# Banded attention with a gated MLP on one core: constant products taken out and the program listed in another order

## The chip, the core and the metric

The kernel runs on one core of a Trainium2 chip. The core's engines work side by side, each through its own list of instructions in the order of the program: PE (TensorE, matrix products into the eight PSUM banks), DVE (VectorE), ACT (ScalarE), POOL (GpSimd) and SP, whose queue issues the DMAs. An instruction waits on semaphores for what it reads. The metric is the device time of one execution in microseconds; lower is better.

## The reference

Attention over 8 batches and 8 heads, 576 positions, with a band of 128 keys and a bias per head; its result, heads side by side, is the input x of a gated MLP whose gate mixes along the sequence.

```python
scores = scale * q @ k.T                       # per batch and head, 576 x 576, D = 64
scores = where((rel >= 0) & (rel < 128), scores - slope[h] * abs(rel), -1e9)
x = concat_heads(softmax(scores) @ v)          # 8 x 576 x 512
h = gelu_tanh(x @ w_in)                        # 512 -> 1024
u, v = h[..., :512], h[..., 512:]
v_n = (v - mean(v)) / sqrt(var(v) + 1e-6) * g_ln
v_s = einsum('ts,bsd->btd', w_sg, v_n) + b_sg  # along the sequence
out = x + (u * v_s) @ w_out
```

## The kernel before

**Order.** All work is cut into named steps. A string, ORDER (L861 on), lists them; `plan.run` goes through it, and `pin` chains the instructions of each engine in that order. So the string sets the order on every engine, and nothing is moved later. A set of names, ON_VECTOR (L66), says which copies and subtractions run on DVE; the others run on ACT (copies) or POOL (subtractions).

**Attention.** A "two" d (0 to 15, two for each batch) holds four heads. Its steps: q (load q and k of two heads, L250), `*a *b *c` (scores, 48 PE instructions each, L287), `A` and `B` (add the bias and take the row minima, DVE, L320), `e` and `E` (exps, ACT, L324), `R` (sum and reciprocal, DVE, L328 and L329), `s` and `z` (scale, POOL, L337, L342), `t` (transpose, DVE, L351), `Va` and `Vb` (product with v, PE, L383). `La` and `Lb` load `vt`, the values of a batch (L264, L266). The q tiles have two buffers apart from the second two, so q4 and q5 wait for the scores of the first two.

**Into the MLP.** For each pair of heads n (four a batch): x (gather from PSUM, L405, L409), h (round to the upper half, L414), l (the rest, the lower half, L417), k (copy of its tail, L420). All products of the MLP are made of three: upper by upper, upper by lower, lower by upper (L628, L629, L630).

**Weights.** `w_in` comes in eight pieces and `w_out` in four, numbered 0 to 11, as 64-bit floats that the core takes apart: i (load into one of four `wst` buffers, L184), r and d (three ACT instructions, L196, L200, L202), b (DVE, L204), + (POOL, L206; it frees the buffer), H (round, L208), - (lower half, L210). 0 to 3 belong to the v-half of `w_in`, 4 to 7 to the u-half, 8 to 11 to `w_out`. The spatial weights: wl, wH, w- for four pieces, tl, tH, t- for the tail, bl, bH, b- for the bias.

**MLP of batch b.** v-sums (`v`; in batch 0 in pieces w and v, one for each pair), vg (gelu, ACT), nv..b, p, c, h and vn (norm: DVE, POOL, DVE, ACT, DVE), tt, tj, tg, nt, tn (the tail of 64 rows), u-sums and uc (copy to SBUF), ug (one gelu over all of u, 2.1 us on ACT), y-sums (along the sequence, L628 to L630, L777, L778; the first of them needs every vn, tn and w-), gm (gate, DVE), gh and gl (halves, ACT and POOL), O (`w_out`), oa (add x, DVE), D (store). u, y and O steps are named by batch, column block and half of the sequence.

**Constant products.** Steps K0 to K23 are listed, and those in ON_VECTOR (ten) issue six products of a constant with itself into an idle PSUM bank (L574), which nothing reads.

Of the kernel before, what the change touches and what calls it, by code (L numbers as in the profile page):

```python
# [22 lines left out]
def attention_gmlp(  # L23
# [833 lines left out]
    for b in range(B):  # L857
# [8 lines left out]
        bH q6 H4 k1 w22 nv10c w01 nv10p -4 v00 b- nv10h k3 q7 k2 w21 w30 vn01 i5 v02 vg00 nv00b vg02 nv20b nv00c
        nv20c w32 La1 nv00p *c3 nv20p *b3 Rb2 Ea2 ea2 nv00h Ra2 w31 Bc3 sb2 vn00 nv20h vn02 tb2 ec2 v03 vg03 sa2
        nv30b nv30c r5 d5 b5 tl i7 Ac3 ta2 tH tt0 nv30p K15 nv30h Rc2 +5 wl1 H5 vn03 -5 tj0 tg0 Bb3 nt0b Lb1 wl0
        sc2 z2 nt0c nt0p *a3 tc2 wH0 ec3 nt0h K6 Va2 Ab3 tn0 r7 q8 Vb2 Aa3 d7 t- Ba3 x4 b7 +7 x6 eb3 H7 -7 w-0
        q9 K10 *a4 *c4 Eb3 wH1 *b4 u020 Rb3 Ba4 Bb4 sb3 w-1 Ea3 Ec3 u010 i9 ea3 u000 Ab4 u001 u021 r9 uc000 Rc3  # L870
        Ra3 q11 wl2 Aa4 Ea4 wl3 uc020 Bc4 tb3 uc001 uc010 u031 sa3 z3 d9 u030 i11 wH3 sc3 uc031 r11 Ac4 uc021
        tc3 ta3 u011 uc030 b9 Eb4 h6 w-3 wH2 d11 Ec4 Va3 Vb3 +9 x5 w-2 y011 b11 +11 y030 q10 y020 l6 h5 ec4
        uc011 H9 x7 H11 y001 l5 *a5 i10 ug0 h4 y021 y031 h7 eb4 gm030 l7 i8 gm021 ea4 gm011 -11 gm031 -9 l4 gh03
        *c5 y010 gm020 Aa5 r8 r10 d10 gh02 k6 gl02 k4 d8 *b5 k5 Ba5 y000 Ac5 gm001 v12 b8 b10 K13 k7 Ab5 +8 +10
        gl03 Ea5 gm010 tt1 ea5 u120 gm000 v10 H8 Rb4 Bb5 gh01 H10 u100 -10 gh00 q13 -8 gl01 sb4 eb5 tj1 u121 K14
        Bc5 La2 Ra5 gl00 tg1 ec5 uc100 tb4 nt1b nt1p Rc4 nt1c q12 Oa00 Ec5 nt1h u131 O000 Lb2 O020 v13 Rc5 Eb5
        tn1 vg10 uc120 oa020 nv01b vg13 z4 O021 O011 Oa01 K17 u110 oa021 sa5 sc4 nv31b nv01c nv31p nv31c nv01p
        oa011 Rb5 nv01h uc110 vn10 Ra4 u130 u111 O031 nv31h K9 vn13 O001 uc121 uc131 ta5 sa4 oa000 uc130 uc111
        vg12 v11 ta4 oa001 tc4 vg11 oa031 nv11b nv21b Va4 D00 O030 Vb4 sb5 oa030 tb5 D02 z5 nv21p nv11c x10 u101
        sc5 nv11p x8 nv11h tc5 *a6 nv21c uc101 ug1 vn11 Ba6 Aa6 *c6 h10 Va5 O010 h8 Vb5 l8 Bc6 k8 oa010 nv21h  # L880
        vn12 D01 Ac6 y100 x9 y130 Ea6 *b6 D03 q14 x11 ec6 h9 l10 y110 l9 ea6 gm100 gm110 Ab6 Ec6 y101 k9 y131
        gm130 q15 *b7 *c7 gm101 h11 l11 k11 k10 Ra6 y121 tt2 Bb6 Ac7 y111 Ab7 Rc6 tj2 gm131 tg2 nt2b y120 *a7
        nt2p gh10 Bb7 v20 Eb7 gm120 sa6 Eb6 eb6 u200 gm121 Aa7 Ba7 v23 sc6 nt2c gm111 gl10 gh11 u221 gh13 gh12
        nt2h ea7 eb7 gl12 gl11 u230 ta6 v22 gl13 Ea7 Rb6 uc200 tn2 Oa10 vg22 nv22b Oa11 O130 uc221 O100 O101
        nv22c z6 La3 O121 nv22p nv22h vg23 vn22 oa100 u201 nv32b oa101 uc230 sb6 v21 O111 Ra7 Bc7 q16 O120 vg20
# [84 lines left out]
```

## Time and profile before

| | us |
|---|---|
| median of three runs | 608.28 (604.44 to 609.07) |
| the profiled execution | 603.53 |
| its span, first to last instruction | 601.8 |
| PE busy | 571.9 (95%) |
| DVE, ACT, POOL busy | 364.9, 347.6, 219.0 |

An fp32 product of attention stands in the trace as two PE instructions' records, and the ends of matmuls are modelled. The profile gives the granted TensorE clock as a share of full speed (1.00 is 2.4 GHz, 0.50 is 1.2 GHz).

### The profile page before, as it was taken

The page shows a single profiled execution, that of the slowest core. Times are in us where ns is not written, and L with a number is a line of the kernel's source. Part 1 is how long each engine was busy: PE and PEld are TensorE (multiplying, and loading weights), DVE is VectorE, ACT ScalarE, POOL GpSimd, SP SyncE. Part 2 cuts the span into 40 slices and gives each one's busy share as a digit, 9 for nine tenths or more (in the row PEclk, how much of TensorE's full clock was granted, in tenths as well). Part 3 has the DMA queues.
Part 4 walks back from the last instruction along what each step waited for, and adds up shares of the span by engine and source line. Part 5 has one row for each costly group of instructions (what it writes and reads, how often), then busy time and mean ns, then how long its engine had stood idle before and what let it go on. Part 6 is the DMA issues. An engine that isn't in the chain of part 4 may idle for free.

```text
span 601.8 us, 20210 instructions
## 1 busy us (share of the span) xinstructions
PE 571.9 (95%) x8632; PEld 525.4 (87%) x8632; DVE 364.9 (61%) x1253; ACT 347.6 (58%) x948; POOL 219.0 (36%) x206
## 2 busy tenths in 40 slices
PE   9668789998999999999999999999999999999997
PEld 9557579888988899988989899998998899999997
...
GB/s 262 122 189 89 208 136 178 49 116 71 40 43 134 93 21 80 103 104 3 78 83 133 3 112 101 104 84 1 101 62 127 59 9 55 23 0 1 1 40 118
DMA packets 27085, 50.22 MB, mean 83 GB/s; under 512 B 2674, under 2 KB 17010, under 8 KB 26996
## 3 DMA queue, kind: packets, MB, share of 16 engines
...
## 4 chain that ended last, share of the span: by engine, by line
PE 84%; DVE 6%; ACT 4%; DMA 3%; issue 2%; SPq 1%; POOL 0%; ACTq 0%
PE bank L628 21%; PE bank L629 20%; PE bank L630 20%; PE bank L383 9%; PE bank L287 6%; PE bank L574 3%; DMA vt<-v_in 2%; PE bank L778 1%; PE bank L777 1%; DMA qk<-qkT 1%; DVE e L320 1%; PE bank L711 1%; PE bank L713 1%; DVE wo L210 1%; ACT e L324 1%
## 5 line engine op out<-in xcount | busy, mean ns | idle before, releaser
L324 ACT ACTIVATE e<-e,small 128x160 f32<-128x160 f32 (+4 forms) x288 | 115.1, 401 | 10.8 <-DVE small L320 10.5
L337 POOL TENSOR_TENSOR e<-e,small 128x960 f32<-128x960 f32 (+1 forms) x48 | 72.0, 1507 | 33.1 <-DVE small L329 31.5
L320 DVE CUSTOM_DVE_ANT_0 e<-bank,bias 128x160 f32<-128x160 f32 (+4 forms) x288 | 69.4, 298 | 22.3 <-PE bank L287 22.0
L652 POOL TENSOR_TENSOR small<-small 128x1 f32<-128x1 f32 (+1 forms) x40 | 27.4, 687 | 145.8 <-DVE small L649 140.0
L628 PE MATMUL bank<-ws,vn 128*128 128x288 f32 x256 | 77.6, 303 | 0.0
L628 PE MATMUL bank<-xs,wi 128*128 128x288 f32 x256 | 77.2, 301 | 0.2 <-DVE vg L718 0.2
L628 PE MATMUL bank<-g,wo 128*128 128x288 f32 x256 | 76.0, 297 | 1.4 <-ACT u L759 1.4
L383 PE MATMUL bank<-e,vt 32*64 32x160 f32 (+4 forms) x3328 | 63.9, 269 | 13.5 <-DMA vt<-v_in 7.0
L383 PEld LDWEIGHTS bank<-e,vt 32*64 32x64 f32 x3328 | 56.7, 137 | 22.1 <-issue 10.3
L629 PE MATMUL bank<-ws,vn 128*128 128x288 f32 x256 | 75.5, 295 | 0.1
L629 PE MATMUL bank<-g,wo 128*128 128x288 f32 x256 | 75.5, 295 | 0.0
L629 PE MATMUL bank<-xs,wi 128*128 128x288 f32 x256 | 75.4, 295 | 0.0
L630 PE MATMUL bank<-g,wo 128*128 128x288 f32 x256 | 75.4, 294 | 0.0
L630 PE MATMUL bank<-ws,vn 128*128 128x288 f32 x256 | 75.4, 294 | 0.0
L630 PE MATMUL bank<-xs,wi 128*128 128x288 f32 x256 | 75.3, 294 | 0.0
L792 POOL TENSOR_TENSOR g<-u,g 128x576 fp32r<-128x576 f32 x32 | 46.9, 1480 | 45.3 <-ACT g L789 35.7
L287 PE MATMUL bank<-qk 64*32 64x160 f32 (+3 forms) x2304 | 53.3, 297 | 7.6 <-DVE small L320 2.5
L417 POOL TENSOR_TENSOR xs<-xf,xs 128x576 fp32r<-128x576 f32 x18 | 25.5, 1429 | 84.5 <-ACT xs L414 63.9
L351 DVE STREAM_TRANSPOSE e<-e 128x480 f32<-128x480 f32 (+1 forms) x96 | 54.2, 608 | 3.3 <-POOL e L337 3.3
L287 PEld LDWEIGHTS bank<-qk 64*32 64x32 f32 x2304 | 41.0, 110 | 16.3 <-issue 6.6
L784 DVE TENSOR_TENSOR u<-bank,u 128x288 f32<-128x288 f32 x64 | 27.5, 451 | 44.5 <-PE bank L778 39.1
L324 ACT ACTIVATION_READ_ACCUMULATOR e<-e,small 128x1 f32 x288 | 54.0, 187 | 0.0
...
## 6 DMA issues: line engine op xcount, KB each, us to landing
...
```

Source lines behind the costliest of these rows:

```text
L287: insts.append(lambda: nc.tensor.matmul(x[quarter[g]], qk[heads[j], 0, n * Q:(n + 1) * Q], ks, start=True, stop=True))
L320: nc.vector.tensor_tensor_reduce(out=e, in0=x, in1=bs, scale=-1.0 / math.sqrt(D), scalar=3e38, op0=ALU.add, op1=ALU.min, accum_out=self.nm ...
L324: nc.scalar.activation(e, e, AF.Exp, bias=self.nm[:, s], scale=-1.0, accum_out=self.sm[:, s, 0])
L337: nc.gpsimd.tensor_tensor(x, x, r.broadcast_to(list(x.shape)), ALU.mult)
L351: nc.vector.transpose(self.pr[:, a:z], self.pr[:, a:z])
L383: insts.append(lambda x=x, start=(k == 0 and at == 0), stop=(k == 1 and left[i] == 0): nc.tensor.matmul(*x, start=start, stop=stop, skip_g ...
L628: nc.tensor.matmul(dst, ah, bh, start=(first and i == 0), stop=False)
L629: nc.tensor.matmul(dst, ah, bl, start=False, stop=False)
L630: nc.tensor.matmul(dst, al, bh, start=False, stop=(last and i == n - 1))
L652: nc.gpsimd.tensor_tensor(x["rs"][0:rows], x["rs"][0:rows], mhalf[0:rows], ALU.pow)
L784: nc.vector.tensor_tensor(u, st[f"py{f}{i}"][:, 0:S2], u, ALU.mult)
L792: nc.gpsimd.tensor_tensor(st[f"g{f}"][:, 1, :], st["u"][:, f, :], st[f"g{f}"][:, 0, :].bitcast(F32), ALU.subtract)
```

## The change

The loop that adds the constant products is gone, and with it their steps. ON_VECTOR and ORDER are others from end to end; the steps are otherwise the same, with the same instructions.

```diff
@@ -64,9 +64,9 @@
     ON_VECTOR = set("""
...
-        k28 x29 l29 k29 x30 x31 H0 H1 -1 r2 -3 -4 -5 H6 -6 H7 -7 -8 -9 H10 -10 -11
+        l0 k0 x1 h1 l1 x2 l2 h3 l3 l4 k4 l5 l6 k6 x7 l7 h8 k8 l9 x10 h10 k10 x11 h11 l11 h12 l12 x13 l13 l14 k14
...
@@ -847,8 +847,6 @@
     WI_AT = [3.0, 8.0, 16.0, 26.0, 36.0, 41.0, 46.0, 51.0]
     WS_AT = 56.0
     WO_AT = 70.0
-    for k in range(24):
-        add_warm(k)
     for d in range(len(twos)):
         add_two(d)
@@ -858,76 +856,75 @@
     ORDER = """
-        K7 K8 q0 i1 K23 r1 K11 q1 K21 d1 i0 b1 r0 q2 *b0 d0 K12 Bb0 Ab0 +1 H1 q3 Eb0 *a0 -1 i2 *c0 *b1 b0 Ba0 +0
...
+        i0 i6 r0 q1 d0 r6 b0 d6 q0 +0 H0 *b0 -0 b6 +6 Ab0 i1 *a0 r1 Bb0 H6 -6 d1 b1 eb0 +1 Aa0 q2 i7 Eb0 Ba0 Rb0
...
```

The lists of instructions show where three things now stand. First SP's queue, from the start of the program. `wst` are pieces of weights, `qk` loads of q and k, `vt` the values of batch 0. Before:

```order
L250 DMA qk<-qkT 128x1152
L184 DMA wst<-w_in 128x512
L250 DMA qk<-qkT 128x1152
L184 DMA wst<-w_in 128x512
L250 DMA qk_168<-qkT 128x1152 x2
L184 DMA wst<-w_in 128x512
L250 DMA qk<-qkT 128x1152
L184 DMA wst<-w_in 128x512
L264 DMA vt<-v_in 32x6x256 x4
```

and now:

```order
L184 DMA wst<-w_in 128x512 x2
L250 DMA qk<-qkT 128x1152 x2
L184 DMA wst<-w_in 128x512
L250 DMA qk_215<-qkT 128x1152
L184 DMA wst<-w_in 128x512
L250 DMA qk_215<-qkT 128x1152
L184 DMA wst<-w_in 128x512
L264 DMA vt<-v_in 32x6x256 x4
```

Five pieces of weights (0, 6, 1, 7, 5) now stand ahead of `vt` in place of four (1, 0, 2, 3), and the third pair's q (q5, the `qk` load just two rows ahead of `vt`) has moved behind it.

Second, ACT's first work, where a decode is L196, L200, L202 and the exps of the first two are L324 into `e_75`. Before, after the load of the exp table:

```order
L196 ACTIVATE wst<-wst 128x512
L200 ACTIVATE vg<-wst 128x512
L202 ACTIVATE wst<-wst 128x512
L196 ACTIVATE wst<-wst 128x512
L200 ACTIVATE vg<-wst 128x512
L202 ACTIVATE wst<-wst 128x512
L324 ACTIVATE e_75,small<-e_75,small 128x160 x13
```

and now:

```order
L196 ACTIVATE wst<-wst 128x512
L200 ACTIVATE vg<-wst 128x512
L202 ACTIVATE wst<-wst 128x512
L208 CAST wi<-vg 128x512
L196 ACTIVATE wst<-wst 128x512
L200 ACTIVATE vg<-wst 128x512
L202 ACTIVATE wst<-wst 128x512
L324 ACTIVATE e_75,small<-e_75,small 128x160 x6
L196 ACTIVATE wst<-wst 128x512
L200 ACTIVATE vg<-wst 128x512
L202 ACTIVATE wst<-wst 128x512
L324 ACTIVATE e_75,small<-e_75,small 128x160 x7
```

A third decode (and a rounding) has moved ahead of the first exp, and a fourth between the first six and the rest.

Third, PE where the first y-sum of batch 0 begins (L628 with `ws` and `vn`). Before it follows the value products of the fourth two:

```order
L383 MATMUL bank<-e_76,vt 64x32 x4
L383 MATMUL bank<-e_76,vt 64x96 x4
L383 MATMUL bank<-e_76,vt 64x64 x8
L383 MATMUL bank<-e_76,vt 64x32 x8
L628 MATMUL bank<-ws,vn 128x288
L629 MATMUL bank<-ws,vn 128x288
```

and now it follows a v-sum of batch 1 (v12):

```order
L629 MATMUL bank<-wi,xs 128x512
L630 MATMUL bank<-wi,xs 128x512
L628 MATMUL bank<-wi,xs 128x512
L629 MATMUL bank<-wi,xs 128x512
L630 MATMUL bank<-wi,xs 128x512
L628 MATMUL bank<-ws,vn 128x288
L629 MATMUL bank<-ws,vn 128x288
```

Scores of the sixth two (`*c5 *b5 *a5`), four v-sums and three u-sums of batch 1 now stand ahead of it.

Over the whole program the counts on DVE, ACT and POOL change thus: 11 of 18 lower halves l and 3 of 4 lower halves of spatial weights go from POOL to DVE, six gathers x from DVE to ACT, one r from POOL to ACT, and ACT has two table loads less.

## Rows read from the trace of the kernel before

**Rows 1.** Windows, two stretches: length, busy of PE, PEld, DVE, ACT, POOL, clock, DMA, GB/s

```profile
0.00:92.00 92.00, 72.12 (x1521) 60.37 (x1521) 65.35 (x264) 62.52 (x189) 42.64 (x49) 0.89 0.57 165
150.00:601.80 451.80, 444.43 (x6435) 413.72 (x6433) 262.80 (x863) 236.30 (x617) 144.44 (x132) 1.00 0.22 64
```

**Rows 2.** Windows, line L574 alone (constant products): PE, PEld busy, clock, DMA, GB/s

```profile
0.00:15.00 15.00, 13.01 (x60) 12.88 (x60) 1.00 0.72 263
...
sum 105.00, PE 22.83 PEld 22.39; mean PE 3.26 PEld 3.20
```

**Rows 3.** Timeline of the first 35 us: start, length, engine, line, operation [idle before <- releaser]

```profile
6.52 0.65 ACT L196 ACTIVATE wst<-wst 128x512 int32<-128x512 uint32 x1 [4.29 <-DMA wst<-w_in]
7.07 0.64 ACT L200 ACTIVATE vg<-wst 128x512 f32<-128x512 f32 x1
7.75 0.65 ACT L202 ACTIVATE wst<-wst 128x512 int32<-128x512 int32 x1
8.43 0.69 DVE L204 SCALAR_TENSOR_TENSOR vg<-vg,wst 128x512 int32<-128x512 int32 x1 [4.06 <-ACT wst L202]
9.22 0.67 ACT L196 ACTIVATE wst<-wst 128x512 int32<-128x512 uint32 x1 [0.82 <-DMA wst<-w_in]
9.27 1.29 POOL L206 TENSOR_TENSOR vg<-vg,wst 128x512 int32<-128x512 int32 x1 [2.59 <-DMA wst<-w_in]
...
13.86 1.85 PE L287 MATMUL bank<-qk 64*32 64x160 f32 x48
15.82 0.32 DVE L320 CUSTOM_DVE_ANT_0 e<-bank,bias 128x160 f32<-128x160 f32 x1 [6.70 <-PE bank L287]
...
21.54 0.33 SPq L250 DMA_DIRECT2D qk<-qkT  x1
...
23.43 4.00 SPq L264 DMA_DIRECT2D vt<-v_in  x6
...
31.72 6.70 PE L383 MATMUL bank<-e,vt 32*64 32x160 f32 x117 [7.02 <-DMA vt<-v_in]
```

**Rows 4.** Chain of waits, first 110 us: start, length, what ran or was waited for

```profile
0.92 13.01 PE bank L574 x60
...
24.87 9.43 DMA vt<-v_in
34.34 4.08 PE bank L383 x84
```

**Rows 5.** Windows by granted clock, columns as in rows 1

```profile
28.00:38.00 10.00, 6.00 (x110) 4.01 (x118) 7.79 (x28) 8.33 (x33) 8.88 (x8) 0.50 1.07 223
38.00:75.00 37.00, 28.89 (x648) 23.08 (x643) 26.92 (x92) 26.80 (x71) 11.65 (x11) 1.00 0.55 149
76.00:85.50 9.50, 8.63 (x186) 7.34 (x194) 9.28 (x29) 5.61 (x10) 6.13 (x7) 0.50 0.45 159
```

**Rows 6.** Chain of waits, 300 to 330 us: prices of PE's work at full clock

```profile
301.45 0.13 PE bank L628
...
316.49 1.80 PE bank L383 x87
318.30 0.98 PE bank L287 x47
...
329.02 0.92 PE bank L713 x4
```

**Rows 7.** Timeline of PE where batch 0's first y-sum begins

```profile
109.50 0.40 PE L628 MATMUL bank<-ws,vn 128*128 128x288 f32 x1
```

**Rows 8.** Groups by form: count | busy us, mean ns | idle before, releasers

```profile
L324 ACT ACTIVATE e<-e,small 128x160 f32<-128x160 f32 x224 | 93.0, 417 | 10.8 <-DVE small L320 10.5
...
L417 DVE TENSOR_TENSOR xs<-xf,xs 128x576 fp32r<-128x576 f32 x14 | 11.0, 806 | 2.8 <-ACT xs L414 2.7
...
L337 POOL TENSOR_TENSOR e<-e,small 128x960 f32<-128x960 f32 x32 | 60.0, 1880 | 27.2 <-DVE small L329 25.6 <-ACT u L759 0.8 <-PE bank L630 0.7
L417 POOL TENSOR_TENSOR xs<-xf,xs 128x576 fp32r<-128x576 f32 x18 | 25.5, 1429 | 84.5 <-ACT xs L414 63.9 <-DVE xs L414 20.6
```

More of the change, by code (lines that the diff above doesn't have):

```diff
@@ L866, in attention_gmlp @@
[L866 to L885, printed above, removed]
@@ new lines, in attention_gmlp @@
+        r7 d7 q3 i5 *c0 H1 La0 i3 -1 b7 *b1 Ea0 Bc0 Ac0 Bb1 ea0 sb0 Ra0 +7 tb0 *a1 Ba1 *c1 ec0 Ec0 r5 sa0 Rc0
+        Ea1 H7 d5 Aa1 Ab1 ta0 eb1 z0 sc0 Lb0 tc0 b5 Bc1 -7 r3 Ac1 +5 Va0 q5 Vb0 d3 q4 *a2 H5 ea1 ec1 *c2 Eb1 b3
+        -5 Ra1 Ec1 +3 x2 H3 Rb1 sa1 Ba2 Ac2 Rc1 h2 sb1 i2 ta1 tb1 r2 x0 i4 d2 -3 h0 *b2 i10 r10 z1 d10 Bc2 sc1
+        b2 Aa2 tc1 +2 H2 l0 b10 Va1 Ec2 ea2 q6 -2 Vb1 l2 gb Bb2 Ea2 Ra2 q7 *c3 Ac3 Ab2 w20 w22 r4 x1 w10 w00 x3
+        +10 sa2 h1 *b3 d4 b4 h3 l3 Eb2 H10 *a3 i11 i8 w02 l1 La1 Bc3 Lb1 w12 Aa3 +4 H4 w11 -4 ec2 -10 eb2 Rb2
@@ new lines, in attention_gmlp @@
+        l7 l5 Bc5 wl1 nv00b Ea4 u131 k7 nv20p ea4 Bb5 nv00p nv00c nv00h nv20c wH1 u121 vn00 Ec4 nv20h wH3 v13
+        Ba5 Ab5 v10 w-0 ug0 vn02 v11 t- tj0 tg0 w-3 nt0b nt0c bl Ac5 bH b- nt0p wl2 nt0h wH2 u100 w-1 tn0 w-2
+        vg10 Aa5 nv01b k4 nv01c v12 Ra4 k5 y030 y031 Rc4 gm030 y021 sa4 vg11 eb4 y001 gm031 Eb5 gm021 Eb4 nv11b
+        nv11c sc4 gm001 y000 y010 Ea5 Rb4 y020 gm000 nv11p y011 k6 gm020 z4 sb4 eb5 gh00 nv01p ea5 gh03 tt1 gh02
+        nv11h gm011 gm010 u120 nv01h gh01 gl03 gl00 Rb5 Ec5 gl02 gl01 vn10 u130 uc100 vg12 vn11 O020 nv21b uc120
@@ new lines, in attention_gmlp @@
+        vg13 u111 Oa01 uc121 tb4 nv31b O021 nv31p nv21c Oa00 Ra5 uc131 nv31c nv21p La2 uc111 O000 oa021 ta4
+        nv31h u110 nv21h q13 vn13 ec5 oa000 vn12 Rc5 O001 tj1 oa001 uc110 tc4 q12 O031 tg1 u101 oa020 z5 nt1b
+        O030 oa031 Lb2 sb5 D02 uc130 nt1p nt1c Va4 O010 oa010 uc101 nt1h oa030 sa5 Vb4 ug1 *b6 tn1 x8 D00 y120
+        ta5 sc5 x10 y110 tc5 *c6 tb5 y101 Bb6 *a6 Ac6 O011 gm110 gm120 Bc6 gm101 ec6 D03 h8 Aa6 oa011 h10 y121
+        l10 l8 Ba6 ea6 Va5 y100 Eb6 Ec6 Vb5 k10 gm121 Ab6 gm100 D01 x11 y111 gm111 k8 eb6 h11 q14 l11 x9 gh10
@@ new lines, in attention_gmlp @@
+        q21 eb9 nv13b sb8 nv03h ea9 nv13p nv13c tb8 vn30 nv13h ec9 u310 O211 Ea9 O210 sa8 uc331 oa230 vn31 tj3
+        Ec9 tg3 ta8 oa210 nt3b oa221 Ra9 z8 nt3p nt3c Rc9 O201 u301 sc9 v33 nt3h uc310 O220 z9 tc8 tn3 v32 oa201
+        Oa20 sa9 O200 oa211 vg33 oa220 q20 uc301 oa200 D21 O231 D20 vg32 u320 uc320 Va8 nv33b nv23b nv33c Eb9
+        oa231 u330 nv33p Vb8 ta9 u321 Rb9 nv33h uc330 *c10 nv23c sb9 nv23p D22 tc9 u311 D23 tb9 x16 nv23h x18
+        Ac10 vn32 h18 Va9 uc311 vn33 Vb9 uc321 x17 h17 x19 y310 y321 ug3 l17 y320 k17 gm321 l18 Bc10 h16 y300
@@ new lines, in attention_gmlp @@
+        nv06h vn60 Ab15 Eb14 ea15 vg63 vg62 k27 eb15 ec15 Rb14 nv36b O520 O510 sb14 nv36p O501 Ba15 nv26b u621
+        Eb15 Ea15 oa510 O511 u620 uc600 nv36c Ra14 uc621 Rb15 nv26p nv26c O521 k25 tt6 Rc14 oa501 uc610 sc14
+        nv36h Ec15 Ra15 nv26h O531 sa14 oa520 tb14 vn63 vn62 u601 Rc15 oa521 oa500 tj6 ta14 oa531 z15 u630 z14
+        uc620 tg6 sa15 sc15 Lb7 D52 u631 sb15 Va14 uc631 oa511 tc14 O530 Vb14 nt6b tc15 nt6c ta15 nt6p nt6h
+        uc601 u611 tn6 y601 x28 D50 D51 tb15 x30 oa530 h28 uc611 Va15 y611 Vb15 h30 D53 y600 uc630 x29 y621 x31
@@ new lines, in attention_gmlp @@
+        h29 l28 y630 l29 y620 h31 ug6 k29 k28 l31 l30 k31 k30 tt7 gm620 gm601 y631 tj7 tg7 v73 y610 nt7b nt7c
+        gm621 v71 gm611 gm610 gm631 gh62 gm600 nt7p nt7h tn7 gh60 u720 gm630 u731 vg73 u721 gh61 gl60 gl62 gh63
+        vg71 gl61 nv37b gl63 Oa60 v72 u700 uc700 O621 O600 nv17b nv37c Oa61 v70 nv17c nv37p nv37h nv17p uc720
+        vn73 u701 vg70 uc721 nv07b oa600 nv17h O601 u710 O620 vn71 vg72 oa601 nv27b nv27p nv07p O630 u730 nv07c
+        nv07h O631 vn70 oa620 nv27c nv27h u711 oa630 vn72 uc731 uc710 uc701 uc730 uc711 y700 O610 y721 y710
```

91 lines of the change are left out of this document (40 added, 51 removed).

## The prediction

> **What bounds the kernel now.** I read three stretches first [rows 1]. From 150 us to the end TensorE is busy in 444.4 of 451.8 us: there it is the bound, ACT and DVE work about half the time, and another order has at most 7 us to win. In the first 92 us TensorE is busy 72.1 us, but its busy time holds the constant products, 22.8 us up to 105 us [rows 2]; it does useful work in about half of that stretch. ACT (62.5 us) and DVE (65.4 us) are not full there either. So the opening waits in chains, and the chain of waits says which [rows 4]: 13.0 us of constant products, then the load of `vt` until 34.34, then products at half the usual pace.
>
> The timeline shows how it hangs together [rows 3]. The second load of the program has landed by 6.52, where ACT begins the first decode, the fourth at 9.22. Both loads of q and k for the first scores are among these four, so the scores could start at about 9.2; they start at 13.86, behind the constants. DVE stands 6.70 us for them. The load q5 stands ahead of `vt` on SP and needs the buffers that the first scores release: SP issues it at 21.54 and `vt` from 23.43, and TensorE's first value products sit on that load until 34.34 [rows 3, 4].
>
> **How I count.** A useful TensorE step has a full-clock price: a score burst of 48 products 0.98 us (47 in 0.98), V in two parts 1.55 and 1.75 (87 products in 1.80), a 512-wide product 0.23 (four in 0.92), a 288-wide one 0.133 [rows 6]. The time of a step less the prices of all useful steps ahead of it is what the opening has lost. Before the first y-sum at 109.50 [rows 7] stand 15 score bursts, 4 V pairs, 16 v-pieces of three wide products, 8 u-sums of 12 and the tail sum of 8: 14.7 + 13.2 + 10.9 + 12.8 + 1.9 = 53.5 us. Lost: 109.5 - 53.5 = 56.0 us.
>
> In the changed order 18 score bursts, 4 V pairs, 16 v-pieces, 11 u-sums, 4 whole v-sums of batch 1 and the tail sum stand ahead of the first y-sum: 17.6 + 13.2 + 10.9 + 17.6 + 10.9 + 1.9 = 72.1 us. The question is when that y-sum can start.
>
> **The change, part by part.**
>
> *Constants out, loads turned round.* SP now issues i0, i6, q1, q0 first. Two loads take 9.22 - 6.52 = 2.7 us, so one takes 1.35: i0 lands at 5.2, i6 at 6.5, q1 at 7.9, q0 at 9.2. ACT decodes i0 from 5.2 to 7.1 (three instructions, 1.9 us from 6.52 to 8.43), DVE joins (0.69), POOL adds (1.29) [rows 3]: +0 ends at 9.2 and frees the buffer for i5, behind which `vt` now stands; q5 stands behind `vt`. `vt` is issued at about 9.7 in place of 23.43. Nine loads are ahead of it (to about 17), and its own 0.8 MB lands by about 22. Gain at the first scores 4.6 us, at `vt` more than 10.
>
> *The walk to the first u-sum.* I put the instructions of DVE, ACT and POOL one behind the other as they stand, each not before what it reads. The exps take 0.41 each, the scaling on POOL 1.8 [rows 8]. TensorE at half clock: first burst 9.2 to 11.1 (1.85 as in [rows 3]). Minima for it end at 12.8, its exps at 14.9, reciprocal 16.3, scaling 18.1; the second half's reciprocal is at 20.1, its scaling at 21.9, the transpose at 25.0. So V0 starts at 25.0 (was 31.7, in fact 34.3), after `vt`. At half clock it ends at 31.6 (was 41.6). x2 is on DVE until 32.8, the transposes of pair two end at 37.4 and 40.6, V1 ends at 42.4 (was 52.6), l1 at 49.4, -4 at 52.1. The first u-sum starts at 52.2 with 24.4 us of work ahead of it: lost 27.8. ACT has meanwhile decoded u's and v's weights in the waits it had before.
>
> *From there to the first y-sum.* TensorE has work without a stop until l5 (DVE, 86.5), which batch 1's u131 waits for; then 16 us more until about 101. ACT has, up to the rounding wH2 that the y-sum needs, 88 us: 84 exps (33), 12 decodes (23), and 32 for table loads, gathers, roundings, gelus and norms, each by the usual distance from its start to the next one's. From 5.2 and never waiting it ends at 92 (1.5 are done before). DVE's list up to w-2 is 85.5 us. The walk, with the waits that I see, puts w-2 and so the y-sum at 102.5: lost 30.4, a gain of 25.6. The other end: ACT no fuller than before. There it was busy 62.5 of the 85.5 us from its first decode to 92 [rows 1, 3], 73%; 86.6 / 0.73 + 5.2 = 124, lost 52, gain 4. I take 107: my walk leaves out hand-overs and each wait that meets another, but the two big holes (constants, `vt`) that made up a good part of the other 27% are gone. Lost 107 - 72.1 = 34.9, gain **21.1 us**.
>
> *Lower halves and gathers.* 11 of 18 lower halves leave POOL (1.43 each) for DVE (0.81) [rows 8], 3 of the spatial weights' too; six gathers leave DVE for ACT; one r leaves POOL for ACT. DVE gains about 4 us of work in sum, ACT as little, POOL loses 21. In the body DVE is busy 262.8 of 451.8 us [rows 1], so I cost it at nothing; its cover is DVE's idle time, and where DVE is full, in the opening, it is in the walk.
>
> *The body's order.* Same steps, same prices. Before it holds 7.4 us of idle TensorE [rows 1]. I cost the new one the same; bounds: 7 us less, or, at the 3.3 us of one gelu with its table load for each of seven batches, 23 more. I take zero since ACT and DVE have half their time free there.
>
> *The clock.* The constants ran for 13 us, and the scores after them took 1.85 us per burst against 0.98 late in the run [rows 3, 6]: they did not bring the fast clock by then, though the page prints 1.00. Later the granted clock is 0.50 in 28 to 38 and 76 to 85.5 us and 1.00 between and after [rows 5]; each fall came behind a stretch in which TensorE had stood (25 to 31.7) or run thin products. So I cost the removal at nothing beyond the half-clock prices in the walk. The Trainium skill speaks against this change: "TensorE: Matmul & The Clock Gate" (section "Why this matters for your kernels") asks for a TensorE kept busy without gaps, else the array returns to half rate. By that rule the new opening, thinner until 52 us, would run at half clock; that is the rival below.
>
> **Sum.** 601.8 - 21.1 = 580.7 us of span. Around the span lie 603.5 - 601.8 = 1.7: 582.4. The three runs shown lie 0.9 to 5.5 above the profiled one; I add 2.5 for that and say **585 us**.
>
> **The rivals.** (A) The forecast, first y-sum at 102 to 115: 580 to 593. Chance 0.60, and 0.06 for quicker still. (B) ACT and DVE wait as often as before, y-sum at 116 to 124: gain 4 to 12, 594 to 602; for it speaks that 73% was reached by the same kinds of steps, against it that SP's late `vt` and the constants caused much of it. 0.20. (C) The body gives it back: a stop of some 2 to 3 us in each of seven batches, in ACT's queue ahead of a gelu, takes 14 to 21 us: 599 to 606, mostly no change. 0.08; against it speaks ACT's 236 of 452 us. (D) Slower, the clock: all 72.1 us ahead of the y-sum at half rate is 144.2 + 9.2 = 153, lost 81, a loss of 25: 629 us. It decides from the point where the y-sum starts after 134 us (lost 62). Speaking for it: TensorE has 24 us of work in its first 43. Against it: wide products ran at granted 1.00 from 38 to 75 us [rows 5], and busy at half rate it has no gaps left. 0.06.
>
> Two more mechanisms are inside A's width: `vt` at the mean rate of before (263 GB/s over the first 15 us [rows 2], so 5.8 MB at 22 us, and by its slow landing as late as 31) costs up to 6; a wl2 that lands late delays w-2 by about 3.
>
> A measurement of this kernel can tell about 1% from no change, 6 us. Faster by more than that (under 602.2): A, the quicker case and most of B, 0.84. Within: 0.10. Slower: 0.06. The range leaves out D, the late part of C and the quickest case: **574 to 601**.
>
> **What would show it.** The first scores at about 9.2 and V0 at 25 (later by `vt`: the loads are the bound); first u-sum near 52; first y-sum at 102 to 115, the term on which all hangs; ACT over 80% busy from 34 to 105 us; no fall of the granted clock after 60 us; TensorE idle under 10 us after the first y-sum. Wrong it would be if ACT and DVE stand in turns from 40 to 100 us, or if the body's idle TensorE grows past 20 us.

## The result, and the profile after

The changed kernel takes 585.11 us (median of 4 runs, 584.70 to 585.71); the kernel before, beside it, 607.38. The ratio is 0.9639, 95% interval 0.9598 to 0.968. The profiled execution took 585.49 with a span of 583.7. The forecast was 585.

It was right in the sum and wrong in three of its terms, which cancel, and that is luck:

| | before | forecast | after |
|---|---|---|---|
| first y-sum starts | 109.50 | 107 | 116.62 |
| work ahead of it | 53.5 | 72.1 | 72.1 |
| lost until then | 56.0 | 34.9 | 44.5 |
| from there to the end | 492.3 | 473.7 | 467.1 |
| span | 601.8 | 580.7 | 583.7 |

(473.7 is 492.3 less the 18.6 us of work that now stand ahead of the first y-sum.) The opening gave 11.5 us where 21.1 were counted, the rest 6.6 where nothing was. And the median stands 0.4 below the profiled run, where 2.5 above it had been allowed for. As gains, the opening was put 9.6 us too high, the rest 6.6 and the step from profile to median 2.9 too low.

The windows of the kernel after, columns as in [rows 1]: the two stretches shown there, the one in which ACT was to be over 80% busy, and what is behind the first y-sum.

```profile
0.00:92.00 92.00, 68.00 (x1704) 55.90 (x1704) 76.23 (x308) 73.63 (x232) 47.42 (x53) 0.89 0.67 198
150.00:583.70 433.70, 427.12 (x6336) 398.76 (x6334) 255.63 (x834) 232.69 (x618) 130.76 (x118) 1.00 0.23 66
...
34.00:105.00 71.00, 59.65 (x1353) 49.91 (x1338) 63.44 (x221) 56.35 (x167) 30.62 (x28) 0.95 0.43 118
116.60:583.70 467.10, 460.52 (x6581) 431.58 (x6579) 277.11 (x882) 254.28 (x681) 148.23 (x134) 1.00 0.22 64
```

Against [rows 1], PE's 68.0 us of the first 92 hold no constant products, and DVE and ACT do 11 us more each. From 34 to 105 us ACT is 79% busy, DVE 89%. Behind the first y-sum PE stands 6.6 us (8.9 before, from 109.50 on).

The timeline of the kernel after, the lines that answer to [rows 3] and [rows 7]:

```profile
5.06 0.67 ACT L196 ACTIVATE wst<-wst 128x512 int32<-128x512 uint32 x1 [2.83 <-DMA wst<-w_in]
...
9.51 1.89 SPq L264 DMA_DIRECT2D vt<-v_in  x4
9.79 4.60 PE L287 MATMUL bank<-qk 64*32 64x160 f32 x144 [9.79 <-DMA qk<-qkT]
...
26.20 5.05 PE L383 MATMUL bank<-e,vt 32*64 32x160 f32 x189 [0.48 <-DVE e L351]
...
116.62 0.29 PE L628 MATMUL bank<-ws,vn 128*128 128x288 f32 x1
```

Scores start at 9.79 (13.86 before), `vt` is issued at 9.51 (23.43), and V0 waits at 26.20 for a transpose and no longer for `vt` (31.72, then to 34.34). Up to here the walk holds within 1.2 us. The first u-sum came at 60.9, not 52.2, and there the opening had lost 36.5 us (60.9 - 24.4) in place of 27.8.

### The profile page after: what moved, and what is told of

Its sections match the earlier page's. It is cut to its first block, busy times and chain, and to the rows that moved or that the text cites. A ratio compares the mean times of both kernels' runs of the same rounds, so it can differ in the third digit from the quotient of the medians.

```text
span 583.7 us, 19971 instructions
## 1 busy us (share of the span) xinstructions
PE 549.3 (94%) x8512; PEld 505.0 (87%) x8512; DVE 376.4 (64%) x1258; ACT 348.1 (60%) x956; POOL 200.4 (34%) x191
## 4 chain that ended last, share of the span: by engine, by line
PE 75%; ACT 5%; DVE 5%; issue 1%; POOLq 0%; POOL 0%; ACTq 0%
PE bank L628 21%; PE bank L629 19%; PE bank L630 19%; PE bank L383 7%; PE bank L287 4%; ACT e L324 2%; PE bank L778 1%; PE bank L777 1%; DVE vg L655 1%; PE bank L711 1%; DVE vn L663 1%; PE bank L713 1%; DVE e L320 1%; DVE e L351 1%; ACT L324 1%
## 5 line engine op out<-in xcount | busy, mean ns | idle before, releaser
L324 ACT ACTIVATE e<-e,small 128x160 f32<-128x160 f32 (+4 forms) x288 | 115.2, 403 | 13.0 <-DVE small L320 12.5
L337 POOL TENSOR_TENSOR e<-e,small 128x960 f32<-128x960 f32 (+1 forms) x48 | 70.2, 1471 | 38.4 <-DVE small L329 27.6
L320 DVE CUSTOM_DVE_ANT_0 e<-bank,bias 128x160 f32<-128x160 f32 (+3 forms) x288 | 69.8, 298 | 16.6 <-PE bank L287 16.3
L628 PE MATMUL bank<-xs,wi 128*128 128x288 f32 x256 | 77.1, 301 | 1.6 <-DVE small L320 0.9
L628 PE MATMUL bank<-ws,vn 128*128 128x288 f32 x256 | 77.6, 303 | 0.5 <-DVE u L784 0.5
L628 PE MATMUL bank<-g,wo 128*128 128x288 f32 x256 | 75.9, 296 | 0.3 <-ACT vg L701 0.3
L287 PE MATMUL bank<-qk 64*32 64x160 f32 (+3 forms) x2304 | 55.7, 302 | 20.3 <-DMA qk<-qkT 11.5
L287 PEld LDWEIGHTS bank<-qk 64*32 64x32 f32 x2304 | 43.2, 112 | 29.8 <-DMA qk<-qkT 11.8
L792 POOL TENSOR_TENSOR g<-u,g 128x576 fp32r<-128x576 f32 x32 | 47.4, 1498 | 59.9 <-ACT g L789 38.8
L383 PEld LDWEIGHTS bank<-e,vt 32*64 32x64 f32 x3328 | 53.4, 134 | 12.5 <-issue 6.5
L383 PE MATMUL bank<-e,vt 32*64 32x160 f32 (+4 forms) x3328 | 57.8, 265 | 5.8 <-DVE e L351 2.9
L628 PE MATMUL bank<-wi,xs 128*128 128x512 f32 x128 | 52.4, 410 | 2.4 <-DVE small L320 2.4
L324 ACT ACTIVATION_READ_ACCUMULATOR e<-e,small 128x1 f32 x288 | 54.4, 189 | 0.0
```

The costliest lines, as they stand in the source:

```text
L287: insts.append(lambda: nc.tensor.matmul(x[quarter[g]], qk[heads[j], 0, n * Q:(n + 1) * Q], ks, start=True, stop=True))
L320: nc.vector.tensor_tensor_reduce(out=e, in0=x, in1=bs, scale=-1.0 / math.sqrt(D), scalar=3e38, op0=ALU.add, op1=ALU.min, accum_out=self.nm ...
L324: nc.scalar.activation(e, e, AF.Exp, bias=self.nm[:, s], scale=-1.0, accum_out=self.sm[:, s, 0])
L337: nc.gpsimd.tensor_tensor(x, x, r.broadcast_to(list(x.shape)), ALU.mult)
L383: insts.append(lambda x=x, start=(k == 0 and at == 0), stop=(k == 1 and left[i] == 0): nc.tensor.matmul(*x, start=start, stop=stop, skip_g ...
L628: nc.tensor.matmul(dst, ah, bh, start=(first and i == 0), stop=False)
```

## Experiments

"First y-sum" and "behind it" (from there to the end) are of the profiled execution of each kernel. "Stops" are the waits of PE in it that the profile puts down to "issue", that is, to nothing that it shows, ahead of the first y-sum and behind it; they are taken up under "Constants put back". All ratios are to the kernel before on the same chip.

| kernel | us | ratio, 95% | first y-sum | behind it | stops |
|---|---|---|---|---|---|
| before | 607.38 | 1 | 109.5 | 492.3 | 6.5, 0.5 |
| before without constants | 594.11 | 0.9794 (0.9757 to 0.9831) | 97.8 | 492.8 | 4.2, 1.3 |
| before, vt first | 603.06 | 0.9933 (0.9909 to 0.9958) | 106.8 | 494.5 | 4.3, 0 |
| before, both | 592.87 | 0.9776 (0.9754 to 0.9798) | 98.8 | 492.3 | 8.1, 1.0 |
| before without constants, new places | 598.22 | 0.9878 (0.9842 to 0.9913) | 98.8 | 496.2 | 4.3, 1.0 |
| after | 585.11 | 0.9639 (0.9598 to 0.968) | 116.6 | 467.1 | 3.4, 1.4 |
| after, vt late | 589.10 | 0.9734 (0.9685 to 0.9784) | 118.0 | 467.0 | 5.0, 1.2 |
| after, x1 first | 586.01 | 0.9685 (0.9643 to 0.9726) | 115.8 | 466.7 | 5.6, 1.1 |
| after, lower halves to POOL | 585.28 | 0.9666 (0.962 to 0.9712) | 116.5 | 468.4 | 5.1, 1.4 |
| after, body's old places | 589.32 | 0.9733 (0.9694 to 0.9773) | 116.8 | 470.9 | 4.0, 1.4 |
| after, q first | 588.35 | 0.971 (0.9654 to 0.9765) | 120.0 | 468.2 | 5.9, 1.3 |
| after, 1 constant | 587.94 | 0.9709 (0.9664 to 0.9754) | 116.9 | 468.6 | 6.9, 1.6 |
| after, 3 constants | 592.64 | 0.978 (0.973 to 0.983) | 117.3 | 473.2 | 8.3, 5.2 |
| after, 6 constants | 600.63 | 0.9902 (0.9873 to 0.9932) | 121.9 | 477.2 | 4.4, 9.0 |

The kernels with the order of before have 53.5 us of work ahead of the first y-sum, those with the new order 72.1, so their columns from the first y-sum on compare within a family only.

Differences of times are those of the medians. The kernel before, measured beside each set of runs, had medians from 605.5 to 607.4 us. By the ratios the other kernels with the new order stand 1.0 to 1.9 us further behind the changed kernel than by their medians (with six constants 0.5).

### The constants and the loads, in the order of before

Without constants:

```diff
-    for k in range(24):
-        add_warm(k)
-        K7 K8 q0 i1 K23 r1 K11 q1 K21 d1 i0 b1 r0 q2 *b0 d0 K12 Bb0 Ab0 ...
+        q0 i1 r1 q1 d1 i0 b1 r0 q2 *b0 d0 Bb0 Ab0 ...
```

> The kernel before with nothing changed but the constant products taken out (their 24 steps and the loop that declares them). Forecast's theory: the first scores go from 13.86 to about 9.2 us, but vt still stands behind q5 on SP, which waits for *c0; it is issued some 4 to 5 us earlier (18.5 to 19.5) and V0 starts near 29.5 to 30.5 instead of 34.3, later stops are partly the same: 4 to 6 us faster than before. Rival (the constants earn their time by raising the granted clock): the scores run at half clock longer, the first of them at 1.7 to 1.9 us as before or slower, and the time is the same within 1 us or longer. Rival (other engines carry the opening, so that an earlier start only waits elsewhere): first scores near 9.2 but the first y-sum within 2 us of 109.5; less than 2 us faster.

12.7 us, twice what the best of the three had. PE's timeline of this kernel:

```profile
5.00 0.76 PE L287 MATMUL bank<-qk 64*32 64x160 f32 x8 [5.00 <-DMA qk<-qkT]
7.83 3.22 PE L287 MATMUL bank<-qk 64*32 64x160 f32 x90 [2.07 <-DMA qk<-qkT]
...
21.63 1.54 PE L383 MATMUL bank<-e,vt 32*64 32x160 f32 x4 [4.37 <-DMA vt<-v_in]
24.15 6.78 PE L383 MATMUL bank<-e,vt 32*64 32x160 f32 x185 [0.98 <-DMA vt<-v_in]
...
97.80 0.40 PE L628 MATMUL bank<-ws,vn 128*128 128x288 f32 x1
```

With q0 at the head of SP's queue the scores start at 5.00, not at 9.2, 8.9 us before those of [rows 3]. V0 starts 10.1 us earlier and the first y-sum 11.7, and from the u-sums to the last product every step is 11 to 12 us earlier. So the opening was one chain behind the constants. Not all of the 11.7 us need be theirs: this kernel also has 2.3 us less of stops ahead of its first y-sum (4.2 for 6.5). The loss of the opening is now 97.8 - 53.5 = 44.3 us: as much as the whole change leaves, 44.5.

`vt` first:

```diff
-        ... ea0 Rb0 q5 H0 ... Rb1 La0 Ea1 ...
+        ... ea0 Rb0 La0 q5 H0 ... Rb1 Ea1 ...
```

> The kernel before with one move: the load of vt stands ahead of q5 on SP, as in the changed kernel; the constants stay. Forecast's theory: vt is issued by about 14 instead of 23.43 us and lands before the V products want it, so that their wait (7.0 us for this load) goes and V0 starts at 29 to 31.7; 3 to 5 us faster. Rival (opening bound by DVE and ACT): V0 starts earlier, the first y-sum does not; less than 1.5 us faster.

3.7 us by the medians, as forecast; V0 starts at 28.8. The profiled execution is only 0.5 us shorter than that of the kernel before: its first y-sum is 2.7 us earlier, and 2.2 go again behind it.

Without constants and with `vt` first:

> The kernel before with both: no constant products, and vt ahead of q5 on SP. This is the opening's removal without the new order of the other steps. Forecast's theory: the two add to 9 to 12 us (first scores near 9.2, V0 near 25 to 26). Rival (new order does the work): 2 to 6 us, and the rest of the 22 us between the two kernels is the order's.

13.9 us, 1.2 more than without constants alone. That is within the spread of those runs (592.3 to 596.1 us), and in the profiled executions the first y-sum comes 1.0 us later. Without constants `vt` is issued at 13.76 even behind q5, and V0 waits 5.4 us for it in all; with both, V0 waits 0.2 us for it, but the stops ahead of the first y-sum are 8.1 us, not 4.2. So the two don't add, and how much of the load's gain went into stops is open.

### What is left: places and order

The kernel before without constants, with the changed kernel's ON_VECTOR:

```diff
-        K2 K6 K7 K8 K11 K12 K15 K18 K21 K23 l0 h1 l1 x2 l2 x3 l3 x5 h5 x6 k6 l7 h8 l8 x9 h9 k9 x10 k11 x13 h13
+        l0 k0 x1 h1 l1 x2 l2 h3 l3 l4 k4 l5 l6 k6 x7 l7 h8 k8 l9 x10 h10 k10 x11 h11 l11 h12 l12 x13 l13 l14 k14
...
```

> The kernel before without its constant products, and with every step that has a choice of engine on the engine that it has in the changed kernel (lower halves, copies, weight steps); the order of the steps stays that of before. It divides the rest of the change (9.0 us by the medians, 594.1 to 585.1; 6.9 by the spans, 590.6 to 583.7) into places and order. Theory that the places give some 4 us whatever the order (giving them back in the changed kernel cost 4.2): 589 to 591 us. Rival (places and order were searched together, and the new places fit only the new order): 594 us or more. Rival (what is left is where the stops of PE's stream fall, since the stream stays that of the kernel before without constants): body within 1 us of that kernel's, 593 to 595 us.

4.1 us slower than without the new places, all but 1 us of it behind the first y-sum. The new places lose in the old order: of the 13.8 us that PE stood there (9.4 with the old places), 5.8 were waits for the gates (gm), which empty the banks of the y-sums and stand on DVE among the moved work. With the old places PE had no such wait. PE's waits by line and releaser (sum in us, times, longest):

```profile
PE bank L629 <- DVE u L785: 5.8, 3, 2.5
PE bank L384 <- ACT xs L415: 1.5, 1, 1.5
```

The other way round, the places of x, h, l and k of pairs 4 to 15 taken back in the changed kernel:

```diff
-        ... h8 k8 l9 x10 h10 k10 x11 h11 l11 h12 l12 x13 l13 l14 k14 ...
+        ... h8 l8 x9 h9 k9 x10 k11 x13 h13 x14 h14 l14 ...
```

> The changed kernel with the lower halves and copies of the body (x, h, l and k of pairs 4 to 15) on the engines that they have in the kernel before, order unchanged. The stretch behind the first y-sum took 467.1 us against 492.3 before, of which 6.5 us are less loss. Theory that the new places of these steps gave it: 3 to 7 us slower than the changed kernel, all behind the first y-sum. Rival (the order, or where the PE stream's stops fall, gave it): within 1.5 us, with the same stops on PE.

4.2 us slower, 3.8 of them behind the first y-sum. Of these, 1.2 are one wait for a q load; such a wait also came in the kernels with lower halves on POOL (1.1) and with one constant (0.9). So the places are worth some 3 to 4 us with their own order and cost as much with the other.

```profile
116.80:587.70 470.90, 461.54 (x6581) 431.54 (x6579) 281.09 (x892) 251.84 (x676) 157.18 (x142) 1.00 0.23 65
```

Against the window of the changed kernel, PE stands 9.4 us in place of 6.6, and DVE's work is only 4 us more.

### The opening of the changed kernel

The forecast costed lower halves on DVE at nothing. All 21 of the opening back on POOL:

```diff
-        l0 l1 l2 l3 l4 l5 l6 l7 -0 -1 -2 -3 -4 -5 -6 -8 -9 -11 w-1 w-2 w-3
```

> The changed kernel with the 21 subtractions of lower halves that stand on DVE in the opening (l0 to l7, the weights' minus steps but two, w-1 to w-3) on POOL instead, order unchanged. Forecast's costing at nothing: within 1.5 us of the changed kernel. Theory that the moved work is what gave the opening its gain, since POOL takes 1.4 to 1.9 us for one where DVE takes 0.7: the first y-sum at 120 to 128 us instead of 116.6, 4 to 11 us slower. Rival (DVE, stretched beside POOL, sets the opening): the first y-sum earlier than 115, 2 to 5 us faster.

No change by the median, 585.28, and 1.6 us slower by the ratio, inside the intervals. Up to the first y-sum DVE's busy time fell from 99.3 to 82.1 us and POOL's rose from 52.1 to 81.0, and that sum started at 116.5. So DVE, 85% busy there, does not set the opening by its work alone. A small gain from a lighter DVE is not excluded: this opening has 1.7 us more of stops than that of the changed kernel and runs for 30.6 us at half clock in place of 23.9.

Where did the walk go wrong? The timeline of the kernel after between V1 and l1:

```profile
43.74 0.48 PE L287 MATMUL bank<-qk 64*32 64x160 f32 x8
45.93 0.46 PE L287 MATMUL bank<-qk 64*32 64x160 f32 x5 [1.71 <-DMA qk<-qkT]
47.73 1.81 PE L287 MATMUL bank<-qk 64*32 64x160 f32 x35 [1.34 <-issue]
48.24 0.32 DVE L320 CUSTOM_DVE_ANT_0 e<-bank,bias 128x160 f32<-128x160 f32 x1 [1.66 <-PE bank L287]
49.23 0.62 DVE L405 COPY xf<-bank 128x448 f32<-128x448 f32 x1
50.56 0.53 ACT L405 COPY xf<-bank 128x448 f32<-128x448 f32 x1 [4.72 <-DVE xf L409]
54.06 3.50 DVE L417 TENSOR_TENSOR xs<-xf,xs 128x576 fp32r<-128x576 f32 x2
56.91 0.51 PE L287 MATMUL bank<-qk 64*32 64x160 f32 x16 [0.70 <-issue]
```

The scores `*c3` wait for their q, and then once more for nothing that the profile shows; DVE's minima of these scores (Ac3) stand ahead of x1, x3 on ACT waits 4.72 us for that, and l3 and l1, which the first u-sum needs, come out at 57.6 in place of 49.4. But PE itself had come no further: from V1's end on it stood 3.75 us, 1.71 for q7 and 1.34 and 0.70 in two stops, ran at half clock from 47.4 to 54.2, and came to w11, its first product that needs l1, at 58.84, 1.3 us after l1. So x1 was put ahead of Ac3:

```diff
-        ... q7 *c3 Ac3 Ab2 w20 w22 r4 x1 w10 ...
+        ... q7 *c3 x1 Ac3 Ab2 w20 w22 r4 w10 ...
```

> The changed kernel with x1 (the transposed sums of the second pair, which x3, l3, l1 and the first u-sum wait for) ahead of the softmax table step Ac3 on DVE, which stands at 48.2 us waiting for scores that wait for q7. Theory that the late q6 and q7 cost the opening through this order: x3 and the first u-sum (60.9 us) come 2 to 4 us earlier, and the first y-sum 1 to 4 us; 581 to 584 us. Rival (DVE's whole work sets the opening, 85% busy to the first y-sum, so that an order only moves its waits): within 1 us of the changed kernel.

x3, l3 and l1 came 1.4 to 1.5 us earlier, the first u-sum 1.4 later, the first y-sum 0.8 earlier, and the time is within 1 us. Behind 57.5 us the clock fell to half for 3.4 us. What was won until then went into a stop on PE, at the place where the changed kernel stops for 0.70 us, so that PE went on only 0.2 us earlier than there:

```profile
56.72 0.51 PE L287 MATMUL bank<-qk 64*32 64x160 f32 x16 [2.67 <-issue]
```

`vt` late again, behind q5:

```diff
-        ... r7 d7 q3 i5 *c0 H1 La0 ... Va0 q5 ...
+        ... r7 d7 q3 i5 *c0 H1 q5 La0 ... Va0 ...
```

> The changed kernel with one move undone: the second pair's third q/k load (q5) stands ahead of vt on SP again, so that vt waits behind a load that waits for the scores *c0 (ending 14.4 us). Forecast's theory: vt is issued at about 14.5 to 15 instead of 9.51 us, is late for V0 (wanted at 26) by 0 to 4 us, since the 4.9 to 6.1 us of a load and the weights queued with it bring it in between 22 and 29: 0 to 3 us slower than the changed kernel (585 to 588 us). Rival (what the runs on the kernel before suggest, where vt first gave 3.7 us with the constants and 1.2 without): no difference over 1 us.

4.0 us slower by the medians, but its runs lie in two pairs, 586.7 and 587.5 at a granted clock of 0.985, 590.8 and 591.0 at 0.971. The profiled one is of the first pair. Its `vt` is issued from 15.29 on in place of 9.51, and V0 starts at 26.26 (26.20) without a wait for it. PE then stops inside V0, u131 comes 3 us late (99.5 for 96.5), the first y-sum 1.4:

```profile
34.70 0.78 PE L383 MATMUL bank<-e,vt 32*64 32x64 f32 x19 [3.43 <-issue]
```

At the same product the changed kernel stops for 1.41 us and the one with lower halves on POOL, whose `vt` is early, for 2.80. So this is one of the stops told of below, and that `vt` came too late is not shown.

The kernel without constants had its first scores at 5.0, this one at 9.8. So the first two q loads were put ahead of the weights:

```diff
-        i0 i6 r0 q1 d0 r6 b0 d6 q0 +0 H0 *b0 ...
+        q0 q1 i0 i6 r0 d0 r6 b0 d6 +0 H0 *b0 ...
```

> The changed kernel with the first two q/k loads (q0, q1) at the head of SP's queue, ahead of the weight loads i0 and i6, instead of behind them. In the kernel before without constants, where q0 stands first, the first scores start at 5.0 us; here they start at 9.79. Theory (a rigid chain from the first scores): scores at 5 to 5.5, V0 2 to 5 us earlier than 26.2, the first y-sum 2 to 4 us earlier; 581 to 583 us. Rival (DVE, 85% busy to the first y-sum, sets the opening; the weights that come later then hold it up): V0 up to 2 us earlier and the first y-sum within 1.5 us of 116.6; 584 to 586 us.

3.2 us slower, which neither theory had. The timeline shows one reason:

```profile
5.80 3.42 PE L287 MATMUL bank<-qk 64*32 64x160 f32 x88 [0.67 <-DMA qk<-qkT]
7.08 0.67 ACT L196 ACTIVATE wst<-wst 128x512 int32<-128x512 uint32 x1 [4.86 <-DMA wst<-w_in]
9.05 0.69 DVE L204 SCALAR_TENSOR_TENSOR vg<-vg,wst 128x512 int32<-128x512 int32 x1 [4.68 <-ACT wst L202]
11.86 0.69 DVE L210 TENSOR_TENSOR wi<-vg,wi 128x512 fp32r<-128x512 f32 x1 [2.11 <-ACT wi L208]
12.46 0.69 DVE L204 SCALAR_TENSOR_TENSOR vg<-vg,wst 128x512 int32<-128x512 int32 x1
13.07 0.32 DVE L320 CUSTOM_DVE_ANT_0 e<-bank,bias 128x160 f32<-128x160 f32 x1
13.94 2.37 PE L287 MATMUL bank<-qk 64*32 64x160 f32 x39 [4.71 <-DVE small L320]
```

The scores run at 4.4 to 9.2, but their minima stand on DVE behind two decodes whose weights now land 2 us later (7.08 for 5.06). The first minimum is at 13.07, in the changed kernel at 11.74, and V0 starts 1.4 us later (27.61). The rest of the 3.4 us at the first y-sum is not followed up; this opening also has 2.5 us more of stops and 3.4 us more at half clock (27.3). With its lists as they are, the changed order did not gain from q first.

### Constants put back: an effect that was not looked for

Six constants ahead of and between the first scores of the changed kernel, as before (their names in ON_VECTOR too):

```diff
+    for k in (7, 8, 11, 12, 21, 23):
+        add_warm(k)
...
-        ... q0 +0 H0 *b0 -0 b6 ...
+        ... q0 +0 H0 K7 K8 K23 K11 K21 *b0 K12 -0 b6 ...
```

> The changed kernel with six constant products put back where before has them, five ahead of the first scores and one behind them, and nothing else changed. Forecast's theory: the first scores come at about 13.5 to 14.5 us instead of 9.8, and the opening hands on most of it: 3 to 5 us slower than the changed kernel (588 to 590 us). Rival (clock): fewer half-clock stretches in the first 110 us (granted clock over 0.90 in it) give the time back; 583 to 586 us. Rival (the end of the opening is set by DVE): less than 1.5 us slower.

15.5 us slower, against 3 to 5 expected. The first y-sum is 5.3 us later, about what the forecast's theory says. But 10.1 more go behind it, where order and work are those of the changed kernel. PE's timeline there, with all stops that the profile puts down to "issue", that is to nothing that it shows, no engine and no load:

```profile
163.47 0.46 PE L288 MATMUL bank<-qk 64*32 64x160 f32 x4 [1.20 <-issue]
181.44 0.31 PE L384 MATMUL bank<-e,vt 32*64 32x32 f32 x7 [0.73 <-issue]
249.98 0.92 PE L384 MATMUL bank<-e,vt 32*64 32x96 f32 x50 [1.27 <-issue]
307.02 0.99 PE L384 MATMUL bank<-e,vt 32*64 32x96 f32 x55 [1.25 <-issue]
364.66 0.82 PE L384 MATMUL bank<-e,vt 32*64 32x96 f32 x37 [0.98 <-issue]
390.30 0.40 PE L630 MATMUL bank<-ws,vn 128*128 128x288 f32 x1 [0.71 <-issue]
473.97 0.26 PE L288 MATMUL bank<-qk 64*32 64x32 f32 x5 [2.85 <-issue]
```

Together 9.0 us; the changed kernel has one such stop behind its first y-sum:

```profile
174.51 0.70 PE L383 MATMUL bank<-e,vt 32*64 32x64 f32 x39 [1.40 <-issue]
```

They fall in the middle of a step: the last is five products before the end of a burst of 144. The table of DMA queues shows PE's likely supplier (columns: packets, MB, share of 16 engines):

```profile
q8 instruction: 66, 1.08, 0.8%
```

PE's program in the changed kernel is 17,077 instructions long (a weight load and a product count one each, an fp32 product two of each); over 66 packets that is 259 for each. If these packets bring it, a stop should fall at fixed numbers of the program, whatever step stands there. One and three constants in the 9.8 us in which PE waits for its first load shift the program by 24 and 72 instructions and delay nothing (the loop and the names in ON_VECTOR as above, for K7, or for K7, K8 and K23, all ahead of `*b0`):

> The changed kernel with one constant product (six small products, about 1.4 us) ahead of the first scores, in the 9.8 us in which PE waits for the first q/k load, so that it delays nothing by itself. With six of them back the body behind the first y-sum lost 10 us more than in the changed kernel, in stops on PE inside score and V steps that wait for no engine. Theory that these stops are PE's instruction stream being loaded (66 fetches of 16 KB each in the table of DMA queues), and that a shift of the stream by a few instructions moves them in and out of the dense score steps: first scores at 9.8 as now, first y-sum within 2 us of 116.6, and the body's stops change place, in the same steps earlier by the same number of instructions; the sum anywhere from 2 us faster to 10 slower. Rival (the constants themselves, or the clock, cost the body): body within 1 us of 467.1.

> The changed kernel with three constant products ahead of the first scores (4.3 us of work in the 9.8 us wait). Theory of the instruction stream: first scores at 9.8, the stops in the body lie at other places again than with one; the difference to one constant has no sign that the number of constants gives. Rival (the constants' delay of the first scores is what costs, 7 of the 12 to 15 us that they were worth): 585 to 587 us, as without. Rival (work on PE before the scores costs or gives clock): the half-clock stretches in the first 110 us change by over 2 us in sum and the first y-sum with them.

The first scores stay at 9.7 and 9.8, the first y-sum at 116.9 and 117.3. Behind it one constant costs 1.5 us, of which such stops give 0.2 and a wait for a q load 0.9; three cost 6.1, with 5.2 us of such stops against 1.4:

```profile
225.79 0.40 PE L629 MATMUL bank<-xs,wi 128*128 128x288 f32 x1 [1.14 <-issue]
...
244.61 0.43 PE L383 MATMUL bank<-e,vt 32*64 32x32 f32 x14 [1.29 <-issue]
...
301.48 0.53 PE L383 MATMUL bank<-e,vt 32*64 32x64 f32 x19 [1.24 <-issue]
...
358.62 0.24 PE L383 MATMUL bank<-e,vt 32*64 32x32 f32 x1 [1.52 <-issue]
```

Counted in the program, the stops lie at:

| kernel | number of the PE instruction behind the stop (rest after division by 256) |
|---|---|
| after | 5567 (191) |
| 3 constants | 7106 (194), 7873 (193), 9663 (191), 11200 (192) |
| 6 constants | 5058 (194), 5823 (191), 7873 (193), 9663 (191), 11200 (192), 12482 (194), 14784 (192) |

Three numbers are the same in two programs that are shifted against each other, and all twelve rests lie within two of 192. My expectation had it wrong in one point: the stops do not move with the steps, the steps move past the places.

The trace also has the start and the length of each packet of q8, which the views here do not list. All hold 16,384 bytes, 64 for each of 256 instructions. In the 14 kernels together PE has 79 stops, those ahead of the first y-sum included. All lie at a rest of 192 or 193 as counted in the trace, and each ends 1.2 to 1.6 us after the packet with the next 256 instructions has landed. Six of them:

| kernel | packet starts | has landed | PE goes on | stop |
|---|---|---|---|---|
| after | 30.15 | 31.18 | 32.66 | 1.41 |
| after | 54.06 | 55.39 | 56.91 | 0.70 |
| after, x1 first | 53.89 | 55.28 | 56.72 | 2.67 |
| after | 172.12 | 173.07 | 174.51 | 1.40 |
| 6 constants | 247.35 | 248.65 | 249.98 | 1.27 |
| 6 constants | 471.05 | 472.42 | 473.97 | 2.85 |

So PE waits there for its instructions. The second and third rows show why x1 first won nothing: PE came earlier and the packet did not.

The packet for a block of 256 instructions starts about when PE enters the block before (0.65 us later in the median of 915) and takes 0.9 to 2.3 us. Two things make it too late. In 45 of the 79 stops PE got through the block before in 2.0 to 3.8 us; where it took longer and the packet started within 2.4 us, there was no stop. In the other 34 the packet started later than that, and there, as in all 71 cases of so late a start, the other queues kept the core's DMA engines over 70% busy meanwhile. That the packet stood behind their transfers is likely but not shown; 119 packets started in time at such a load.

This is how constants ahead of the first scores cost time behind the first y-sum. The blocks that end at the three numbers which two programs share hold 128 V products each with three and with six constants, and PE takes 2.0 to 2.1 us for one. In the changed kernel 12 to 17 of the 128 are products of the MLP, and PE takes 3.6 to 4.1 us and does not stop.

On this the Trainium skill, "Runtime: NRT & Kernel Launch" (section "Instruction fetch mechanics"), says that each engine refills its instruction memory by a DMA queue of its own in blocks of 256 instructions, and that the cost of a block's end is mostly hidden. The trace agrees on the spacing, and on "mostly": 836 of 915 such places were passed without a stop. The others cost up to 3.65 us at one place, and 9.0 us in sum behind the first y-sum of one program.

The other 2.3 to 2.5 us behind the first y-sum, in either kernel, are not stops: PE's busy time there is 1.8 and 2.3 us longer. With three constants the granted clock falls to 0.51 from 359.4 to 362.8 us, right behind the stop at 358.6; with six it does not fall there.

## Why the prediction was right, and where it was not

**The opening: right in direction, mis-sized, 11.5 us for 21.1.** The forecast put the chance of this (B, y-sum at 116 to 124) at 0.20, against 0.60 for its own case. The steps up to V1 held: `vt` at 9.51 (9.7), V0 at 26.2 (25.0), x2 done at 34.5 (32.8), V1 at 43.8 (42.4). The step that failed is the next, from V1's end to l1: 13.8 us in place of 7.0, and the first u-sum came 8.7 us later than walked. From that u-sum to the y-sum the forecast had 54.8 us (50.3 by the walk and 4.5 on top of it), the trace 55.7. On DVE the walk gave each subtraction its own length, where the two of l3 and l1 took 3.50 us. On PE it had no wait for q6 and q7, no work at half clock behind V1 and no stop for instructions; PE came to its first product with l1 1.3 us later than l1 did. The stops alone are 3.4 us ahead of the first y-sum.

What else sets 116.6 is not settled. x1 earlier, DVE lighter by 17 us, `vt` later, one constant and three: the first y-sum stayed between 115.8 and 118.0. That does not show that these steps cost nothing there, for two other things moved with them. The stops ahead of the first y-sum are 5.0 to 8.3 us in these kernels and 3.4 in the changed one. And the changed kernel, unlike these, has a fall of the clock at v10, shortly ahead of the first y-sum (below): with one constant and with three, v10 started 1.9 and 2.3 us later, and the first y-sum 0.3 and 0.7. Only a later start of scores or minima moved it (120.0 and 121.9). Each wait that was taken away was followed by another.

**Where the opening's gain came from.** The forecast gave it to constants, loads and order together. Taking out the constants alone brings the first y-sum 11.7 us forward, all there is, and 2.3 us of stops went with them. The forecast had the first scores free at 9.2, where the fourth load lands; their q are the first and the third load, and without constants they start at 5.00. The new order of the opening has done its part by putting 18.6 us more work ahead of the first y-sum at the same loss.

**The body: costed at 0, in fact 6.6 us better,** at the edge of the bound of 7. ACT and DVE had half their time free, and still places and order were worth something. 2.3 us are less idle time on PE, 1.4 shorter score bursts (34.3 us for 33 before, 30.0 for 30 after, at 0.98 a burst); the rest is spread over V and v-sums and I have not followed it. Some 3 to 4 hang on the places together with their order. Rival C did not happen. Waits for instructions don't explain it: they are 0.5 us before and 1.4 after.

**Lower halves on DVE: nothing,** not refuted in the opening (585.28 for 585.11, with more stops and more half clock in the one), where its cover was said to be least. In the body the places were not free.

**The clock: right that the constants do not pay.** Granted 0.50 in the first 150 us: before for 20.4 us, without constants 23.8, with the change 23.9 (13.7 + 6.8 + 3.4), with three constants 23.8, with six 17.0. So in the order of before they saved 3.4 us of half clock, some 1.7 us, for 11.7, and six in the new order 6.9, some 3.4 us, for 5.3. "No fall after 60 us" was wrong; the windows of the kernel after at half clock, columns as in [rows 5]:

```profile
16.70:30.40 13.70, 10.13 (x287) 7.77 (x278) 13.32 (x65) 12.95 (x49) 9.14 (x8) 0.50 1.08 285
...
47.40:54.20 6.80, 6.47 (x46) 5.39 (x47) 3.84 (x15) 3.56 (x12) 1.57 (x2) 0.50 1.11 202
...
105.50:108.90 3.40, 3.40 (x10) 2.62 (x9) 3.24 (x9) 2.87 (x3) 0.00 (x0) 0.51 0.00 0
```

The last one follows a stop of 2.41 us ahead of v10, and makes that sum 4.6 us long where 3.0 is usual: from the start of v10 to the first y-sum the changed kernel takes 11.5 us, those with x1 first, body's old places and one constant, which stop there as long and have no fall, 9.9. Rival D, slower by the clock, fell: half clock lasted 3.5 us longer than before, and the first y-sum came at 116.6, not after 134. By the rule of the Trainium skill, "TensorE: Matmul & The Clock Gate" (section "Why this matters for your kernels"), the thinner opening should have run at half rate; it did so for 23.9 of its first 150 us.

**From profile to median.** 1.8 us around the span as counted; the 2.5 for the spread of runs was not there.
